# Local attention scores by 64x32 tiles in a windowed attention and sticky-expert kernel

## The chip, the cores and the metric

The kernel runs on one core of one Trainium2 chip. The core has a matrix engine (TensorE, PE in the profile, with its weight loads as PEld), a vector engine (VectorE, DVE), a scalar engine (ScalarE, ACT), GpSimd (POOL), and a queue engine (SyncE, SP) that issues most transfers to 16 DMA engines. Each engine works its own list of instructions in order; semaphores tie the lists together. The metric is device microseconds for one execution.

## The reference

Eight batches of eight heads hold 512 local tokens and 32 global tokens, with 64 features a head. Global tokens attend to all 544 tokens. A local token attends to the 32 global tokens and to the local tokens at most 32 positions away. The attention output, 512 features a token, goes through a mixture of experts, where a token takes its own best expert or, when its gate is at or over one half, that of the token before.

```
s_ll = scale * matmul(q_l, k_l^T);  s_ll = where(|i - j| <= 32, s_ll, -1e9)
s_lg = scale * matmul(q_l, k_g^T)
out_l = softmax([s_lg, s_ll]) @ [v_g, v_l]
out_g = softmax(scale * matmul(q_g, [k_g, k_l]^T)) @ [v_g, v_l]
x = concat(out_g, out_l)          # 8 x 544 tokens of 512
e = argmax(x @ w_gate) if s == 0 or sigmoid(x @ w_local) < 0.5 else e of token s-1
out = softmax(x @ w_gate)[e] * (relu(x @ w1[e]) @ w2[e])
```

## The kernel before, in words

**Units.** `run` (L419) walks 48 units in a fixed order written out by hand: in each batch four local ones (`l`, one pair of heads each) and two global ones (`g`, two pairs each), in the order l0, l1, g0, l2, g1, l3. In step `s` it scores unit `s` and finishes unit `s-2` (transposes of the probabilities, product with v, division). So a step issues on TensorE: the transposes of unit `s-2` (`l_t`, or `g_t`), the scores of unit `s`, and the products with v of unit `s-2`, in two halves for a local unit (`l_av`), with pieces of later work between them (`fpiece`: transposes of finished rows `f1`, the gates `f2`, `f3`).

**Local scores.** The 512 queries are 16 windows of 32. Each window sees 128 keys: its own block, its two neighbours and the global block, and the host's order with a copy on GpSimd (`prep`, L192, the `kx` tile) puts those 128 columns side by side for every window. For one pair of heads, the 128 rows of q and k are 64 features of one head and 64 of the other. To score both heads in one matmul of 128 rows, `prep` copies q into a tile `qbd`, where a window has 64 columns, 32 a head, and the other head's rows are zero. `l_s` (L225) is called twice a unit, for windows 0 to 7 and 8 to 15. Each call writes one PSUM bank: first a bf16 matmul of an identity with a mask (`mask`) that puts a large negative number where a key is out of reach, then eight score matmuls on top of it, each writing 64 of the 128 partitions. `l_max` (L244) takes the row maximum and subtracts it on VectorE, `l_exp` (L251) is the exponential on ScalarE, `l_t` (L255) transposes on TensorE and copies out on ScalarE, and `l_av` (L264) multiplies with v in 16 matmuls of 32 columns, whose last column gives the sum, and divides on VectorE. Scores use a ring of four banks, transposes and outputs two each.

**What a matmul leaves in the profile.** An f32 matmul with another operand than the identity appears as two records, so the 8 score calls of one half are 16 records.

**Transfers.** All loads go through SP's queue in program order. In a local step it issues the load of q and k for the pair after next (`load`, L171, 4224 bytes a partition in a ring of four `raw` buffers that the experts' weights use later), and v for the next pair (`loadv`, L183, 8320 bytes a partition, ring of five). Each is contiguous per partition. A load into a buffer waits for that buffer's last reader, and every later issue on SP waits with it.

**Row store.** When a batch's rows and gate values are done, `f3k` (L398), a generator that VectorE work is dripped from (`drip`, one piece at a few places of each step), computes routing keys and gate probabilities, then waits six further drips (`lag(F4)`, F4 = 6) and calls `f4` (L405), which issues one store of 1056 KB from the row buffer `xa` (ring of two), four of `xg` and one of `gx` on SP. The last batch's store is issued in `tail`.

**Experts.** From step 44 on the first blocks of the expert part begin among the last units (`moe.pre`): gathers, weight loads, and the split of each weight piece into two parts for full precision. Then the blocks run, each a first product (L1158) and a second (L1169), beside the remainder of the attention (`tail`).

Of the kernel before, what the change touches and what calls it, by code (L numbers as in the profile page):

```python
# [11 lines left out]
I32 = mybir.dt.int32  # L12
# [44 lines left out]
F4 = 6  # L57
# [41 lines left out]
class Attn:  # L99
    def __init__(self, tc, cst, tl, at1, at2, raw, ps, qk, qg, vw, xs):  # L100
        nc = self.nc = tc.nc
        self.tc, self.cst = tc, cst
        self.at1, self.at2 = at1, at2
        self.qk, self.qg, self.vw, self.xs = qk, qg, vw, xs
        self.ld = raw
        self.ps_s, self.ps_t, self.ps_o = ps
        self.xa = ring(tl, [P, 4, ROW], F32, "xa", 2)
        self.xg = ring(tl, [P, 2, D], F32, "xg", 2)
# [5 lines left out]
        self.rs = ring(tl, [P, 2, 2, 1], F32, "rs", 3)  # L114
# [6 lines left out]
        self.pt = ring(at1, [P, 4, 2, 2, 32], F32, "pt", 4)  # L121
        self.qbd = ring(at2, [P, NW, 2, 32], F32, "qbd", NBUF)
# [4 lines left out]
        self.mask = at2.tile([P, 8, 2, 32], BF16, name="mask")  # L127
        self.m0 = at2.tile([P, 2, 32], F32, name="m0")
        self.cur = {}
        self.gens = []  # L130
        self.low = 0
        self.banks = False
        self.npr = 0

    def make_mask(self):
# [8 lines left out]
        nc.vector.tensor_copy(self.mask, m0.rearrange("p (o a) k -> p o a k", o=1).broadcast_to([P, 8, 2, 32]))  # L144
        nc.vector.memset(self.mask[0:64, 0, 0, :], NEG)
        nc.vector.memset(self.mask[64:128, 7, 1, :], NEG)
# [24 lines left out]
    def load(self, b, pr):  # L171
# [5 lines left out]
        nc.sync.dma_start(t, self.qk[b, pr])  # L177
# [5 lines left out]
    def loadv(self, b, pr):  # L183
# [3 lines left out]
        nc.sync.dma_start(v.rearrange("p w c -> p (w c)"), self.vw[b, pr])  # L187
# [4 lines left out]
    def prep(self, u):  # L192
# [3 lines left out]
        q = t[:, 0:SL].rearrange("p (w q) -> p w q", q=32)  # L196
        qbd, kx = u["qbd"], u["kx"] = self.qbd(), self.kx()
        k = t[:, SL:]
        kf = kx.rearrange("p m c k -> p (m c) k")
        if self.npr == 0:  # L200
            nc.scalar.copy(out=qbd[0:64, :, 0, :], in_=q[0:64])
            nc.vector.tensor_copy(qbd[64:128, :, 1, :], q[64:128])
            nc.vector.tensor_copy(kx[:, 1:8, 2, :], k[:, 32:64].rearrange("p (o k) -> p o k", o=1).broadcast_to([P, 7, 32]))
        else:
            self.cp(qbd[0:64, :, 0, :], q[0:64], [[0, NW], [0, 32]])
            self.cp(qbd[64:128, :, 1, :], q[64:128], [[0, NW], [0, 32]])
# [7 lines left out]
    def blank(self, i):  # L214
        nc = self.nc
        qbd, kx = self.qbd.t[i], self.kx.t[i]
        nc.vector.memset(qbd[0:64, :, 1, :], 0.0)
        nc.vector.memset(qbd[64:128, :, 0, :], 0.0)
# [6 lines left out]
    def l_s(self, st, hb):  # L225
        nc = self.nc
        if hb == 0:
            b, pr = st["u"]
            if pr == 0:
                self.cur[b]["xa"] = self.xa()  # L230
                self.cur[b]["xg"] = self.xg()
            st["pe"] = self.pe()
        qbd = st["qbd"]
# [3 lines left out]
        nc.tensor.matmul(mo, self.cst.idb, self.mask[:, 4 * hb:4 * hb + 4], start=True, stop=False, skip_group_check=True)  # L237
        for t in range(4):
            for t2 in range(2):
                w = 8 * hb + 2 * t + t2  # L240
                f = 32 * (3 * (w // 2) + w % 2)
                nc.tensor.matmul(sp[64 * t2:64 * t2 + 64, t], qbd[:, w], kf[:, f:f + P], start=False, stop=True, skip_group_check=True)  # L242

    def l_max(self, st, hb):  # L244
        nc = self.nc
        mx = self.mx()
        nc.vector.tensor_reduce(out=mx, in_=st["sp"], axis=AX.X, op=ALU.max)  # L247
        self.drip()
        nc.vector.tensor_tensor(out=st["pe"][:, 4 * hb:4 * hb + 4], in0=st["sp"], in1=mx.broadcast_to([P, 4, P]), op=ALU.subtract)  # L249

    def l_exp(self, st, hb):  # L251
        pe = st["pe"][:, 4 * hb:4 * hb + 4]
        self.nc.scalar.activation(out=pe, in_=pe, func=AF.Exp, scale=SCALE)  # L253

    def l_t(self, st, hb):  # L255
        nc = self.nc
        tp = self.bank(self.ps_t)
        for i in range(4):
            nc.tensor.transpose(tp[:, i], st["pe"][:, 4 * hb + i], self.cst.idf)
        pt = self.pt()  # L260
        nc.scalar.copy(out=pt.rearrange("p i t h q -> p i (t h q)"), in_=tp)
        st["pts"] = st.get("pts", []) + [pt]

    def l_av(self, st, hb):  # L264
# [4 lines left out]
        pt = st["pts"][hb]  # L269
        o = self.ps_o()[:, 0:2 * VW].rearrange("p (g h c) -> p g h c", h=2, c=D + 1)  # L270
        for g in range(2):
            for h in range(2):
                for w4 in range(4):
                    w = 8 * hb + 4 * g + w4
                    nc.tensor.matmul(o[32 * w4:32 * w4 + 32, g, h], pt[:, 2 * g + w4 // 2, w4 % 2, h, :],
                                     v[:, w, h * (D + 1):(h + 1) * (D + 1)], start=True, stop=True, skip_group_check=True)
        rs = self.rs()
        nc.vector.tensor_scalar(out=rs, in0=o[:, :, :, D:D + 1], scalar1=1e-9, scalar2=None, op0=ALU.add)
# [3 lines left out]
        xo = c["xa"][:, 2 * hb:2 * hb + 2, 2 * D * pr:2 * D * (pr + 1)].rearrange("p g (h c) -> p g h c", c=D)  # L282
        nc.vector.tensor_tensor(out=xo, in0=o[:, :, :, 0:D], in1=rs.broadcast_to([P, 2, 2, D]), op=ALU.mult)
# [114 lines left out]
    def f3k(self, b, rt):  # L398
# [3 lines left out]
        yield from lag(F4)  # L402
        self.f4(b, rt)
# [15 lines left out]
    def run(self, rt, moe):  # L419
# [31 lines left out]
        for s in range(n):  # L451
            nx = units[s]
# [23 lines left out]
            if nl:  # L476
                self.l_s(nx, 0)
# [7 lines left out]
            if nl:  # L485
                self.l_exp(nx, 0)
                self.l_s(nx, 1)
# [17 lines left out]
            if s < 6:  # L505
                self.drip(4)
            moe.pre(s - n)
# [11 lines left out]
        self.drip(1000)  # L519
        moe.tail = self.tail(units[n - 2], units[n - 1], fin, rt, moe)  # L520
# [66 lines left out]
class Route:  # L587
# [4 lines left out]
    def setup(self):  # L592
# [6 lines left out]
        i128 = c.tile([P, P], I32, name="i128")  # L599
# [6 lines left out]
        ik = c.tile([P, NF, E], I32, name="ik")  # L606
# [4 lines left out]
        nl = c.tile([P, P], F32, name="nl")  # L611
# [17 lines left out]
        self.o1 = c.tile([P, NT, P], BF16, name="o1")  # L629
        self.oe = c.tile([P, CA, 2, 2 * NX], BF16, name="oe")  # L630
# [728 lines left out]
def _layout(q_l, k_l, v_l, q_g, k_g, v_g, moe_w_gate, moe_w_local, moe_w1, moe_w2):  # L1359
# [5 lines left out]
    r["qk"] = np.concatenate([tr(q_l), tr(k_l)[..., :32], tr(k_g), tr(k_l)[..., 32:]], axis=3)  # L1365
    g = tr(q_g).transpose(0, 2, 1, 3).reshape(B, 2, D, NP, 1, SG)
# [10 lines left out]
    r["vw"] = np.concatenate(rows, axis=2).reshape(B, NP, P, NW * VW)  # L1377
# [31 lines left out]
```

## Time and profile before

| | |
|---|---|
| median of 3 runs | 744.25 us (742.75 to 746.08) |
| the profiled execution's own time | 743.35 us |
| its span, first to last instruction | 741.6 us |
| TensorE busy | 698.0 us (94%) |
| VectorE busy | 503.9 us (68%) |
| ScalarE busy | 411.6 us (55%) |
| GpSimd busy | 238.1 us (32%) |
| moved by DMA | 178.74 MB, mean 241 GB/s |

Busy time is a mean over the attention part and the expert part, which have different limits. A group in a view is written as line, engine, operation, output<-input tile, shape and count; after the bar stand busy time in us, mean length of one in ns, and the engine's idle time before the group with what ended it. For a matmul, `128*64` is rows by columns of the array that the stationary operand takes, and `128x128` the moving operand. Matmuls overlap, so the distance between two starts says more than the printed length.

### The profile page before, as it was taken

How to read it: one execution, taken by the hardware profiler on the slowest of the kernel's cores; microseconds unless marked ns; L12 is line 12 of the kernel's file. 1: busy time of each engine (PE TensorE's matmuls, PEld its weight loads, DVE VectorE, ACT ScalarE, POOL GpSimd, SP SyncE). 2: the span in 40 equal slices, each digit the busy share in tenths (PEclk: the TensorE clock that was granted, in tenths of full speed). 3: DMA queues.
4: the chain of work that ended last, by engine and by line, in shares of the span. 5: the costliest groups of instructions: out<-in, count | busy, mean ns of one | idle time of the engine just before them, and what ended most of it. 6: DMA issues, size and time to landing. Idle time of an engine off the chain costs nothing. (4 is left out here: it accounts for less than half of the span.)

```text
span 741.6 us, 19626 instructions
## 1 busy us (share of the span) xinstructions
PE 698.0 (94%) x7797; PEld 593.0 (80%) x7797; DVE 503.9 (68%) x1207; ACT 411.6 (55%) x724; POOL 238.1 (32%) x333
## 2 busy tenths in 40 slices
PE   9999999999998988899899999999999999999990
PEld 7777777777677877788889888888888988999880
DVE  7877777779887578876558585575858455745560
ACT  4555555554556744545466665566767445645550
POOL 7534434424244455332041412123232121112120
PEclk9999999999999999999999999999999999999995
DMA  8876786767583775677478797757878667657772
GB/s 325 351 260 235 291 312 240 281 245 271 208 323 121 260 246 196 217 248 208 162 238 295 256 299 237 233 191 244 287 238 289 225 221 235 199 193 243 217 228 75
DMA packets 50575, 178.74 MB, mean 241 GB/s; under 512 B 8733, under 2 KB 10013, under 8 KB 46368
## 3 DMA queue, kind: packets, MB, share of 16 engines
q1 hardware_dynamic: 43456, 155.76, 61.4%
q0 software_dynamic: 6720, 21.36, 8.3%
q8 instruction: 71, 1.16, 0.6%
q14 instruction: 40, 0.33, 0.2%
q10 hardware_dynamic: 288, 0.13, 0.1%
HBM read 158.84 MB, written 19.42 MB: 240 GB/s over the span
## 5 line engine op out<-in xcount | busy, mean ns | idle before, releaser
L1097 DVE TENSOR_TENSOR wp<-raw,wp 128x1024 fp32r<-128x1024 f32 x158 | 198.3, 1262 | 8.4 <-ACT wp L1088 8.1
L1088 ACT CAST wp<-raw 128x1024 fp32r<-128x1024 f32 x176 | 182.8, 1048 | 36.5 <-DMA raw<-in_w_dram 34.3
L1169 PE MATMUL ps<-wp,hh 128*128 128x512 f32 x608 | 195.1, 402 | 0.0
L1158 PE MATMUL ps<-xh,wp 128*128 128x256 f32 x1088 | 157.4, 286 | 14.4 <-DVE hl L1161 7.8
L1158 PEld LDWEIGHTS ps<-xh,wp 128*128 128x128 f32 x1088 | 142.3, 192 | 19.1 <-DVE hl L1161 9.4
L1161 DVE SCALAR_TENSOR_TENSOR hl<-ps,hh 128x256 fp32r<-128x256 f32 x136 | 57.1, 422 | 122.7 <-ACT hh L1160 122.7
L1169 PEld LDWEIGHTS ps<-wp,hh 128*128 128x128 f32 x608 | 109.3, 188 | 21.6
L1112 POOL DMA_INDIRECT xr<-xs,idx x46 | 59.5, 1294 | 207.4 <-PE ps L1123 112.8
L1169 PE MATMUL ps<-wp,hl 128*128 128x512 f32 x304 | 120.3, 396 | 0.0
L1160 ACT ACTIVATE hh<-ps 128x256 fp32r<-128x256 f32 x136 | 51.3, 385 | 85.5 <-PE ps L1158 80.6
L1158 PE MATMUL ps<-xl,wp 128*128 128x256 f32 x544 | 87.8, 284 | 0.0
L1179 POOL DMA_INDIRECT out_dram<-y,tk x38 | 40.8, 1074 | 135.5 <-POOLq L1292 28.9
L190 POOL TENSOR_SCALAR_AFFINE_SELECT qbd<-raw 64x512 f32<-64x512 f32 x62 | 44.5, 717 | 120.5 <-PE ps L242 100.3
L1158 PEld LDWEIGHTS ps<-xl,wp 128*128 128x128 f32 x544 | 75.4, 192 | 0.0
L242 PE MATMUL ps<-kx,qbd 128*64 128x128 f32 x1024 | 71.3, 280 | 1.9 <-issue 1.7
L1169 PEld LDWEIGHTS ps<-wp,hl 128*128 128x128 f32 x304 | 57.1, 188 | 13.6
L242 PEld LDWEIGHTS ps<-kx,qbd 128*64 128x64 f32 x1024 | 55.1, 137 | 12.5 <-issue 8.2
L247 DVE TENSOR_REDUCE mx<-ps 128x4 f32<-128x512 f32 x64 | 43.9, 686 | 29.0 <-PE ps L242 28.8
L253 ACT ACTIVATE pe<-pe 128x512 f32<-128x512 f32 x64 | 40.8, 637 | 29.2 <-DVE pe L249 29.2
L1178 ACT ACTIVATE y<-ps,pp 128x512 f32<-128x512 f32 x38 | 26.0, 685 | 52.6 <-issue 46.3
L1097 POOL TENSOR_TENSOR wp<-raw,wp 128x1024 fp32r<-128x1024 f32 x17 | 43.8, 2578 | 23.5 <-ACT wp L1088 22.1
L249 DVE TENSOR_TENSOR pe<-ps,mx 128x512 f32<-128x512 f32 x64 | 44.1, 688 | 1.6
(214 smaller groups left out, 842.3 us busy)
## 6 DMA issues: line engine op xcount, KB each, us to landing
raw<-in_w_dram SPq DMA_DIRECT2D x179, 512.0 KB, 4.5
v<-in_vw_dram SPq DMA_DIRECT2D x32, 1040.0 KB, 9.5
raw<-in_qk_dram SPq DMA_DIRECT2D x32, 528.0 KB, 7.3
xs<-xa SPq DMA_DIRECT2D x8, 1056.0 KB, 4.8
qgb<-in_qg_dram SPq DMA_DIRECT2D x8, 128.0 KB, 3.8
xr<-xs,idx POOLq DMA_INDIRECT x46, 6.3
out_dram<-y,tk POOLq DMA_INDIRECT x38, 5.4
xs<-xg SPq DMA_DIRECT2D x32, 16.0 KB, 4.0
```

Source lines behind the costliest of these rows:

```text
L190: self.nc.gpsimd.affine_select(out=out, in_=in_, pattern=pat, compare_op=ALU.is_ge, fill=0.0, base=0, channel_multiplier=0)
L242: nc.tensor.matmul(sp[64 * t2:64 * t2 + 64, t], qbd[:, w], kf[:, f:f + P], start=False, stop=True, skip_group_check=True)
L247: nc.vector.tensor_reduce(out=mx, in_=st["sp"], axis=AX.X, op=ALU.max)
L249: nc.vector.tensor_tensor(out=st["pe"][:, 4 * hb:4 * hb + 4], in0=st["sp"], in1=mx.broadcast_to([P, 4, P]), op=ALU.subtract)
L253: self.nc.scalar.activation(out=pe, in_=pe, func=AF.Exp, scale=SCALE)
L1088: nc.scalar.copy(out=hi, in_=raw)
L1097: (nc.gpsimd if pool else nc.vector).tensor_tensor(out=lo, in0=raw, in1=hi.bitcast(F32), op=ALU.subtract)
L1112: self.nc.gpsimd.indirect_dma_start(out=self.xr[j], out_offset=None, in_=src, in_offset=bass.IndirectOffsetOnAxis(ap=self.rt.idx[:, 2 * i ...
L1158: nc.tensor.matmul(ph, a[:, dc, fs], b_[:, dc], start=(n == 0), stop=(n == 11))
L1160: nc.scalar.activation(out=self.hh[:, fc], in_=ph, func=AF.Relu)
L1161: nc.vector.scalar_tensor_tensor(out=self.hl[:, fc], in0=ph, scalar=0.0, in1=self.hh[:, fc].bitcast(F32), op0=ALU.max, op1=ALU.subtract)
L1169: nc.tensor.matmul(py, a[:, fc, js], b_[:, fs], start=(fc == 0 and k == 0), stop=(fc == 7 and k == 2))
```

## The change

**Scores by 64x32 tiles.** `qbd` and its copies and zero fills are gone. `l_s` is called once a unit and writes two banks, one a head, each after its own mask matmul. It then makes 32 calls, window by window and head by head: 64 rows (one head's features, read from q where it was loaded), 32 columns (one window's queries), 128 moving columns (the window's keys). A bank now holds one head's 16 windows, four by partition and four along the bank, where it held eight windows of both heads. `l_max`, `l_exp`, `l_t` and `l_av` go by head instead of by half of the windows; the shapes on VectorE and ScalarE stay 128x512 and 128x256. The mask tile is half as long. Within a step the scores of both heads come before the first product with v.

**Row store.** `f4` is no longer called by the generator. At the end of the probabilities the batch is noted with a step, the present one plus F4[b], 4 for batches 0 to 3 and 0 for 4 to 6, and at the end of a step the stores that are due are issued. `xa` and `xg` get three buffers.

**Layout by the host.** q and k of a pair lie in DRAM as two blocks of 128 x 528 floats (2112 bytes a partition each) instead of rows of 4224 bytes, v as four blocks of 128 x 520 floats (2080 bytes). Each load is still one instruction, and the tiles on chip are filled as before.

**Room.** Three scratch tiles of the routing set-up (`i128`, `nl`, `ik`) move into the tile `o1`, which is filled later.

```diff
-F4 = 6
+F4 = (4, 4, 4, 4, 0, 0, 0)
...
         t = c[("qk", pr)] = self.ld()
-        nc.sync.dma_start(t, self.qk[b, pr])
+        nc.sync.dma_start(t.rearrange("p (c x) -> p c x", c=2), self.qk[b, pr].rearrange("c p x -> p c x"))
...
-        nc.sync.dma_start(v.rearrange("p w c -> p (w c)"), self.vw[b, pr])
+        nc.sync.dma_start(v.rearrange("p (g w) c -> p g (w c)", g=4), self.vw[b, pr].rearrange("g p x -> p g x"))
...
-            self.cp(qbd[0:64, :, 0, :], q[0:64], [[0, NW], [0, 32]])
-            self.cp(qbd[64:128, :, 1, :], q[64:128], [[0, NW], [0, 32]])
...
-        sp = st["sp"] = self.bank(self.ps_s)
-        mo = sp.rearrange("p t (k c) -> p t k c", c=32)[:, :, 0::3, :]
-        nc.tensor.matmul(mo, self.cst.idb, self.mask[:, 4 * hb:4 * hb + 4], start=True, stop=False, skip_group_check=True)
+        sp = st["sp"] = [self.bank(self.ps_s) for _ in range(2)]
+        for h in range(2):
+            mo = sp[h].rearrange("p t (k c) -> p t k c", c=32)[:, :, 0::3, :]
+            nc.tensor.matmul(mo, self.cst.idb, self.mask, start=True, stop=False, skip_group_check=True)
         for t in range(4):
-            for t2 in range(2):
-                w = 8 * hb + 2 * t + t2
-                f = 32 * (3 * (w // 2) + w % 2)
-                nc.tensor.matmul(sp[64 * t2:64 * t2 + 64, t], qbd[:, w], kf[:, f:f + P], start=False, stop=True, skip_group_check=True)
+            for h in range(2):
+                r = slice(D * h, D * h + D)
+                for j in range(4):
+                    w = 4 * t + j
+                    f = 32 * (3 * (w // 2) + w % 2)
+                    nc.tensor.matmul(sp[h][32 * j:32 * j + 32, t], q[r, 32 * w:32 * w + 32], kf[r, f:f + P], start=False, stop=True, skip_group_check=True)
...
         yield from rt.probs(b, c["L"], c["xa"])
-        yield from lag(F4)
-        self.f4(b, rt)
+        self.post.append((self.step + F4[b], b))
...
             if nl:
-                self.l_s(nx, 0)
+                self.l_s(nx)
                 self.l_max(nx, 0)
...
             if nl:
                 self.l_exp(nx, 0)
-                self.l_s(nx, 1)
                 self.l_max(nx, 1)
...
+            while self.post and self.post[0][0] <= s:
+                self.f4(self.post.pop(0)[1], rt)
             moe.pre(s - n)
```

More of the change, by code (lines that the diff above doesn't have):

```diff
@@ L126, in __init__ @@
         self.qgb = ring(at2, [P, NP, 2, 32], F32, "qgb", 2)
-        self.mask = at2.tile([P, 8, 2, 32], BF16, name="mask")
+        self.mask = at2.tile([P, 4, 2, 32], BF16, name="mask")
         self.m0 = at2.tile([P, 2, 32], F32, name="m0")
@@ L133, in __init__ @@
         self.npr = 0
+        self.step = 0
+        self.post = []
     def make_mask(self):
@@ L268, in l_av @@
         v = c["v"][pr]
[L269 to L276, printed above, removed]
+        pt = st["pts"][h]
+        o = self.ps_o()[:, 0:4 * (D + 1)].rearrange("p (t c) -> p t c", c=D + 1)
+        for t in range(4):
+            for j in range(4):
+                nc.tensor.matmul(o[32 * j:32 * j + 32, t], pt[:, t, j], v[:, 4 * t + j, h * (D + 1):(h + 1) * (D + 1)],
+                                 start=True, stop=True, skip_group_check=True)
         rs = self.rs()
-        nc.vector.tensor_scalar(out=rs, in0=o[:, :, :, D:D + 1], scalar1=1e-9, scalar2=None, op0=ALU.add)
+        nc.vector.tensor_scalar(out=rs, in0=o[:, :, D:D + 1], scalar1=1e-9, scalar2=None, op0=ALU.add)
         self.drip(hold=True)
@@ L451, in run @@
         for s in range(n):
+            self.step = s
             nx = units[s]
```

75 lines of the change are left out of this document (36 added, 39 removed).

## The prediction

> **What bounds the kernel now.** I read the page's first part, then a table of stretches, then TensorE's own order of work, then waits and transfers. The kernel has an attention part and an expert part; they meet where the last local score starts, 231.8 us by its group:
>
> ```profile
> L242 PE MATMUL ps<-kx,qbd x1024: 269/273/477, 5.4 to 231.8; 128*64 128x128 f32 x171
> ```
>
> The stretches come first; their columns are the length, each engine's busy time, the granted clock, the DMA engines' busy share, and GB/s.
>
> ```profile
> span 741.6 us, 19626 instructions
> PE 698.0 (94%) x7797; PEld 593.0 (80%) x7797; DVE 503.9 (68%) x1207; ACT 411.6 (55%) x724; POOL 238.1 (32%) x333
> ```
> ```profile
> 0.00:12.00 12.00, 10.44 (x94) 8.42 (x96) 8.92 (x24) 3.50 (x5) 9.20 (x34) 1.00 0.84 325
> 12.00:40.00 28.00, 27.39 (x590) 20.80 (x593) 23.37 (x83) 16.99 (x38) 17.86 (x55) 1.00 0.79 309
> 40.00:160.00 120.00, 119.53 (x2542) 90.98 (x2532) 90.59 (x306) 67.95 (x159) 45.66 (x99) 1.00 0.76 280
> 160.00:232.00 72.00, 67.58 (x1373) 51.28 (x1370) 59.47 (x217) 39.44 (x90) 25.92 (x51) 1.00 0.65 239
> ```
>
> From 40 to 160 us TensorE is busy 119.5 of 120 us: it sets the pace. VectorE is second, at 90.6 (75%). From 160 to 232 us VectorE is at 59.5 of 72 (83%) and TensorE has already 4.4 us free. A count of the score records puts 17 pairs of heads into the first stretch and 9 into the second, here with busy time of TensorE and of its weight loads:
>
> ```profile
> 40.00:160.00 120.00, 37.20 (x544) 29.00 (x544) 1.00 0.76 280
> 160.00:232.00 72.00, 19.85 (x288) 15.35 (x288) 1.00 0.65 239
> ```
>
> 32 records are one pair (8 calls for each of two halves, two records a call). What one step costs TensorE is read from its order of work; the time of a group is the distance from its start to the next start, since the printed length includes a tail under which the next group runs.
>
> ```profile
> 106.69 0.33 PE L338 MATMUL ps<-v,ptg 128*32 128x65 f32 x9
> 106.95 1.09 PE L259 MATMUL ps<-idf,pe 128*128 128x128 f32 x8
> 107.88 0.27 PE L237 MATMUL ps<-mask,idb 128*128 128x256 bf16 x1
> 108.08 1.09 PE L242 MATMUL ps<-kx,qbd 128*64 128x128 f32 x16
> 109.10 0.67 PE L275 MATMUL ps<-v,pt 128*32 128x65 f32 x32
> 109.70 0.28 PE L237 MATMUL ps<-mask,idb 128*128 128x256 bf16 x1
> 109.92 1.09 PE L242 MATMUL ps<-kx,qbd 128*64 128x128 f32 x16
> 110.94 0.67 PE L275 MATMUL ps<-v,pt 128*32 128x65 f32 x32
> 111.53 0.87 PE L327 MATMUL ps<-idf,pg 128*128 128x128 f32 x6
> ```
>
> Eight transposes that fill the array take 107.88 - 106.95 = 0.93 us, 0.116 each for 128 moving columns. Sixteen scores, each on half the array's columns, take 109.10 - 108.08 = 1.02 us, 0.064 each: two column halves run at a time. A step has two such runs, 2.04 us, and two masks (0.20 and 0.22 us).
>
> **The scores.** The edit turns 8 + 8 calls of 128 rows by 64 columns, with half of their stationary operand zero, into 32 calls of 64 rows by 32 columns: 64 records a pair instead of 32, each still streaming 128 columns. Alone, one after another, they would take 64 x 0.116 = 7.4 us. What matters is how many run together. The nearest rows are those with 32-column tiles:
>
> ```profile
> 13.01 1.12 PE L275 MATMUL ps<-v,pt 128*32 128x65 f32 x64
> ```
> ```profile
> 219.03 1.06 PE L366 MATMUL ps<-xT,wgl 128*32 128x512 f32 x8
> 219.91 0.64 PE L275 MATMUL ps<-v,pt 128*32 128x65 f32 x32
> ```
>
> Eight gate records of 512 columns would take 8 x 4 x 0.116 = 3.7 us singly and take 0.88: four at a time, nothing lost. And 64 value records last 1.12 where 32 last 0.67, so a further 32 cost 0.45 us, 0.014 each; alone one costs 0.116 x 65/128 = 0.059: again four. No row shows tiles that share columns but not rows, so the cost is bounded: if only the four column tiles overlap, 64/4 x 0.109 + 0.15 = 1.9 us (a run of 1.02 us holds 8 rounds of two; I take 0.109 a round and 0.15 for ramp and change of shape); if all eight do, 8 x 0.109 + 0.15 = 1.02 us. I take eight: in the rows both two and four tiles side by side reach their full number, the halves of rows hold different heads, and they write different banks (each head has its own). That removes one run: -1.02 us a pair, -32.7 us in 32 pairs; with four it would be -0.15 a pair.
>
> [...]
>
> **Around the scores.** One more row, of POOL's copies of q:
>
> ```profile
> L190 POOL TENSOR_SCALAR_AFFINE_SELECT qbd<-raw 64x512 f32<-64x512 f32 x62 | 44.5, 717 | 120.5 <-PE ps L242 100.3
> ```
>
> The two masks follow each other, so one change of tile shape goes: 0.20 + 0.22 becomes about 0.11 + 0.21, -0.1 a pair, -3.2 us. The two value runs can stand together where no finishing piece falls between them: 0.60 + 0.59 becomes 0.45 + 0.60, -0.15 in about half of the steps, -2.4 us. At the start the second pair's keys no longer wait behind two POOL copies of q (0.72 us each); about -1. Together TensorE sheds 39 us, 1.2 a pair.
>
> **What is late next: VectorE.** Its work a pair does not change: the maximum, the subtraction and the scaling keep their shapes.
>
> ```profile
> L249 DVE TENSOR_TENSOR pe<-ps,mx 128x512 f32<-128x512 f32 x34 | 23.5, 692 | 1.0
> L247 DVE TENSOR_REDUCE mx<-ps 128x4 f32<-128x512 f32 x34 | 23.4, 688 | 18.7 <-PE ps L242 18.7
> L283 DVE TENSOR_TENSOR xa<-ps,rs 128x256 f32<-128x256 f32 x35 | 14.8, 422 | 2.1 <-DMA xs<-xa 1.3
> ...
> L280 DVE RECIPROCAL rs<-rs 128x4 f32<-128x4 f32 x35 | 6.2, 178 | 0.7
> L278 DVE TENSOR_SCALAR rs<-ps 128x4 f32<-128x4 f32 x35 | 5.4, 155 | 1.2 <-PE ps L275 0.9
> ```
>
> From 40 to 160 us TensorE needs 120 - 17 x 1.2 = 99.6 us, against 90.6 for VectorE. In a step with both a local pair to score and one to finish, VectorE has 4 x 0.69 + 2 x 0.75 = 4.3 us beside its small pieces and TensorE now about 4.0 (3.3 and a finishing piece), in steps of the global rows it is the other way round; four banks of scores let one engine run about a step ahead. I charge 3 us: 102.6, a gain of 17.4. From 160 to 232 us TensorE would need 67.6 - 10.8 = 57 us, less than VectorE's 59.5; at 95% VectorE takes 62.6, a gain of 9.4. Before 40 us VectorE (32.3 of 40) allows about 4. The sum is -30.8 before transfers, 8 us less than TensorE alone gives.
>
> **Store and descriptors.** The row store waits in SP's queue for VectorE, and each load behind it waits too:
>
> ```profile
> 52.37 0.38 SPq L187 DMA_DIRECT2D v<-in_vw_dram  x1
> 63.62 0.38 SPq L412 DMA_DIRECT2D xs<-xa  x1
> 64.06 3.22 SPq L416 DMA_DIRECT2D xs<-xg  x4
> 67.37 0.37 SPq L417 DMA_DIRECT2D xs<-gx  x1
> 67.85 1.39 SPq L177 DMA_DIRECT2D raw<-in_qk_dram  x1
> ```
> ```profile
> SPq L412 <- DVE xa L768: 47.2, 5, 11.5
> SPq L1077 <- PE ps L295: 14.3, 2, 9.0
> ```
> ```profile
> POOL qbd L190 <- PE ps L242: 100.3, 23, 8.0
> POOL qbd L190 <- DMA raw<-in_qk_dram: 11.7, 4, 4.3
> ```
>
> No load leaves between 52.4 and 67.9 us; POOL then waited four times for keys (11.7 us), but had 100 us to spare, and TensorE did not stop. So the move earns 0 by itself (up to 2 if it ends small waits), and is cover: with shorter steps the same hold would reach TensorE, at up to 4.3 us a batch. Batches 0 to 3 move four steps back, so the six issues of each store (one row, four xg, one gx, 4 us of SP) stand behind finished data; a third row buffer pays for that. Batches 4 to 6 lose the six drips of delay they had, so SP waits for VectorE as before or longer, with the next q, k and v queued behind. I charge 1 us (0 to 3 x 3).
>
> Descriptors:
>
> ```profile
> v<-in_vw_dram SPq DMA_DIRECT2D x32, 1040.0 KB, 9.5
> raw<-in_qk_dram SPq DMA_DIRECT2D x32, 528.0 KB, 7.3
> xs<-xa SPq DMA_DIRECT2D x8, 1056.0 KB, 4.8
> ```
>
> The row store moves 1056 KB as rows of 528 floats, 2.1 KB each, and lands in 4.8 us, v with its 8.3 KB rows in 9.5: pieces of 2 KB carry this rate, so 0. At the other end, as many bytes in less time raise the DMA share from 0.76 to about 0.76 x 120/103 = 0.89; from there a load can be late. POOL loses 44.5 us of copies that it hid anyway. TensorE now reads q in the loaded buffer, which is free one use later: the fourth weight load waited for the global scores (L295) and will wait for the last local scores, a step later, with the other weight loads behind it. Price 0 to 3 us, taken as 1. The sum: -30.8 + 1 + 1 = -28.8.
>
> **The rivals.** (1) The likeliest: eight tiles at a time, VectorE close behind. 743.35 (the profiled execution, span 741.6) - 28.8 = 714.5; it lies 0.9 under the median of 744.25, so 715.4 for a median; own range 707 to 722. (2) VectorE binds harder: its waits for scores (18.7 of 120 us) stay as they are, because each maximum must follow its scores. Then 90.6 + 18.7 = 109.3 us instead of 120; that 9% over 192 us is 17, with the start 18: 726. For it: VectorE is 83% busy in the second stretch; against: half of its waits are for a second run that goes. [...] (3) The row halves don't overlap: -0.15 - 0.1 - 0.07 a pair, -10 us: 734. Against: side-by-side tiles overlap in full; for: no row shows it. (4) Full gain, both engines hidden: -39: 705. (5) The slower side: going from one row half to the other empties the array, as a change of shape does. The row of the mask gives the price: 0.20 us to the next start for work of 0.11, so 0.09 lost. Sixteen rounds of 0.109 + 0.09 make 3.2 us where two runs took 2.04, +1.15, less 0.17 around them, +1.0 a pair: +31 us, 775. It decides from about 30 ns a change. Against it: all 64 value records run through four tiles without such a gap, though within one set of rows.
>
> **How the numbers follow.** Chances: (1) 0.52, (2) 0.14, (3) 0.13, (4) 0.09, (5) 0.09, and 0.03 that late loads or late weights take back a small gain. The time is that of (1), 715. The range 702 to 736 takes in (1) to (4), 0.88 less their edges. About 0.5% (3.7 us) is what can be told from no change: faster 0.87 (cases 1 to 4 but for an edge), same 0.04, slower 0.09.
>
> **What would show it.** The order of work after: one group of 64 score records in 1.0 us (four at a time: 1.9; emptying: over 3), two masks together, steps about 1.2 us shorter on TensorE, the last score record at about 202 us instead of 231.8. VectorE above 85% from 40 us until there, its waits for scores well below 0.55 us each. SP without a hold of 15 us in batches 0 to 3. The expert part unchanged to about 3 us. I am wrong if the score group takes over 1.3 us, if VectorE stays near 75% while TensorE has gaps, or if TensorE waits for POOL's keys after loads.

## The result, and the profile after

The changed kernel takes 771.27 us (median of 4 runs, 767.73 to 774.64) where the kernel before takes 745.16 (4 runs, 742.75 to 753.18): 1.034 times as long, 95% interval 1.027 to 1.041. The forecast was 715. A profile is of one execution, which can be longer than its kernel's median: 774.64 us here, and further on 756.75 (two new units, median 753.08), 843.88 (split loads, 842.07) and 747.93 (nearly no loads, 738.2). The span of this one is 31.2 us longer than that of before. Most of this lies ahead of the expert part: the last local score starts at 257.6 us instead of 231.8, and what follows it takes 515.2 us instead of 509.8.

The page of the changed kernel, its first lines, the granted clock in 40 slices of the span, and the queue that brings the engines' code:

```profile
span 772.8 us, 21648 instructions
...
PE 684.2 (89%) x8821; PEld 579.1 (75%) x8821; DVE 497.7 (64%) x1202; ACT 410.2 (53%) x723; POOL 194.2 (25%) x271
...
PEclk9999899889999997999999999999999999999996
...
q8 instruction: 79, 1.29, 0.7%
```

TensorE has less busy time than before (684.2 against 698.0) and 1024 matmul records and 1024 weight loads more, 64 instructions a pair. The page of before has this line for the code:

```profile
q8 instruction: 71, 1.16, 0.6%
```

Eight packets more for 2048 more instructions: a packet is a block of 256 TensorE instructions, 1.29 MB / 79 = 16 KB. The stretches of the changed kernel, in the columns of the prediction's table:

```profile
12.00:40.00 28.00, 21.48 (x683) 16.70 (x685) 19.43 (x74) 15.29 (x37) 9.59 (x41) 1.00 0.86 316
40.00:160.00 120.00, 95.88 (x2458) 70.39 (x2455) 72.53 (x257) 56.43 (x133) 17.84 (x52) 0.90 0.66 226
160.00:232.00 72.00, 59.23 (x1662) 44.37 (x1660) 55.73 (x209) 35.86 (x83) 13.14 (x36) 0.95 0.67 229
```

Before, TensorE was busy for 119.5 of the 120 us from 40 to 160; now for 95.9, and VectorE has become emptier with it, 72.5 instead of 90.6. Neither is the bound. What TensorE waits for, between 6 and 258 us (us in total, times, longest):

```profile
PE ps L238 <- issue: 12.9, 7, 4.1
PE ps L269 <- issue: 12.9, 7, 3.5
PE ps L332 <- issue: 4.8, 2, 3.0
PE ps L345 <- DVE xa L277: 4.8, 4, 2.5
```

and the largest entry of the same view of before, 6 to 250 us:

```profile
PE ps L242 <- issue: 1.7, 2, 1.3
```

"issue" is idle time in which the engine waits for nothing that the profile shows. It sits in front of the scores (L238), the products with v (L269) and the global products (L332), the lines with the smallest matmuls, and it is 30.6 us in these three rows. TensorE's order of work shows what such a wait looks like, and beside it a step without one:

```profile
44.51 0.38 PE L231 MATMUL ps<-mask,idb 128*128 128x256 bf16 x2
44.82 0.89 PE L238 MATMUL ps<-kx,raw 64*32 64x128 f32 x43
49.82 0.99 PE L238 MATMUL ps<-kx,raw 64*32 64x128 f32 x21 [4.11 <-issue]
...
59.72 0.38 PE L231 MATMUL ps<-mask,idb 128*128 128x256 bf16 x2
60.03 1.16 PE L238 MATMUL ps<-kx,raw 64*32 64x128 f32 x64
61.12 1.35 PE L269 MATMUL ps<-v,pt 128*32 128x65 f32 x64
```

Sixty-four score records take 61.12 - 60.03 = 1.09 us, as forecast. But the group before stops after 43 records, in the middle of an operation whose operands are all there, and goes on 4.1 us later. In the stretch from 47.3 to 48.4 us, inside this gap, the transfers' view has one instruction packet in a stream of loads:

```profile
DMA packets 204, 0.42 MB, mean 377 GB/s; under 512 B 13, under 2 KB 13, under 8 KB 203
## 3 DMA queue, kind: packets, MB, share of 16 engines
q1 hardware_dynamic: 203, 0.40, 97.9%
q8 instruction: 1, 0.02, 5.0%
```

**TensorE has run out of instructions.** The following is worked out from the single records of the trace, by counting all of TensorE's instructions in it (matmuls, weight loads and the few of its sequencer) from the start and setting the instruction packets beside the count. In both traces a block's packet begins some time after a mark that returns every 256 instructions, and lasts about 1.0 us (0.9 to 1.4). Where TensorE used up the 256 from that mark before the packet had landed, it stopped, each time at the same remainder of the count (193), and went on 1.3 to 1.5 us after the packet's end. Up to 225 us that happens once before the change and 12 times after it (in two of the 12 the packet had landed less than 0.1 us earlier). From the first instruction after the mark to the packet it is 2.2 us in the mean before (5.3 at most) and 2.6 after (6.6 at most). After the change, the waits of over 3 us stand where loads move 240 to 405 GB/s between mark and packet, and with no load in that time it is 0.4 to 1.6 us. The expectations below count from the last instruction before the mark, which takes in a stop at the mark itself; by that count the means are 2.3 and 3.4, and the longest is 7.9.

So the wait itself has grown little. What the change has cut is the time that it must fit into, and that is in the tables: before, 2542 + 2532 records in 120 us are a block every 6.05 us. In the new step (mask, 64 scores, 64 values, with their weight loads) 256 records last about 3 us. A wait of 2.6, a transfer of 1.0 and the 1.4 until TensorE goes on are 5.0 us, which fit into the first and not into the second.

The granted clock falls with the stops: 0.90 from 40 to 160 us, and 1.00 before. In the trace's single clock records it is 1.00 or 0.50; ahead of the last score 0.50 comes in stretches of 3.4 or 6.8 us, 34.1 us in all, and none before the change. Each stretch at half clock begins inside a stop or at most 1.2 us after one.

### The profile page after: what moved, and what is told of

It is laid out like the page before. It is cut to its first block, busy times and chain, and to the rows that moved or that the text cites. A ratio compares the mean times of both kernels' runs of the same rounds, so it can differ in the third digit from the quotient of the medians.

```text
span 772.8 us, 21648 instructions
## 1 busy us (share of the span) xinstructions
PE 684.2 (89%) x8821; PEld 579.1 (75%) x8821; DVE 497.7 (64%) x1202; ACT 410.2 (53%) x723; POOL 194.2 (25%) x271
## 3 DMA queue, kind: packets, MB, share of 16 engines
q8 instruction: 79, 1.29, 0.7%
## 5 line engine op out<-in xcount | busy, mean ns | idle before, releaser
L1167 PE MATMUL ps<-wp,hh 128*128 128x512 f32 x608 | 197.4, 406 | 0.0
L192 POOL TENSOR_SCALAR_AFFINE_SELECT kx<-raw 128x384 f32<-128x384 f32 (+3 forms) x127 | 44.1, 372 | 188.4 <-PE ps L238 131.1
L269 PE MATMUL ps<-v,pt 128*32 128x65 f32 x2048 | 44.4, 231 | 19.6 <-issue 12.9
L269 PEld LDWEIGHTS ps<-v,pt 128*32 128x32 f32 x2048 | 35.9, 115 | 29.7 <-issue 19.5
L238 PE MATMUL ps<-kx,raw 64*32 64x128 f32 x2048 | 42.0, 280 | 13.0 <-issue 12.9
L1095 POOL TENSOR_TENSOR wp<-raw,wp 128x1024 fp32r<-128x1024 f32 x17 | 43.1, 2539 | 21.1 <-ACT wp L1086 18.3
```

What stands on the lines that cost most here:

```text
L192: self.nc.gpsimd.affine_select(out=out, in_=in_, pattern=pat, compare_op=ALU.is_ge, fill=0.0, base=0, channel_multiplier=0)
L238: nc.tensor.matmul(sp[h][32 * j:32 * j + 32, t], q[r, 32 * w:32 * w + 32], kf[r, f:f + P], start=False, stop=True, skip_group_check=True)
L269: nc.tensor.matmul(o[32 * j:32 * j + 32, t], pt[:, t, j], v[:, 4 * t + j, h * (D + 1):(h + 1) * (D + 1)], start=True, stop=True, skip_grou ...
L1095: (nc.gpsimd if pool else nc.vector).tensor_tensor(out=lo, in0=raw, in1=hi.bitcast(F32), op=ALU.subtract)
L1167: nc.tensor.matmul(py, a[:, fc, js], b_[:, fs], start=(fc == 0 and k == 0), stop=(fc == 7 and k == 2))
```

## The experiments

In the expectations theory A is the one of the section above: more instructions, a block of code that waits behind loads, and a TensorE that runs out of them. Its rivals are named where they stand.

**The parts one by one.** Scores alone, with the old layout and the old store:

```diff
-        nc.sync.dma_start(t.rearrange("p (c x) -> p c x", c=2), self.qk[b, pr].rearrange("c p x -> p c x"))
+        nc.sync.dma_start(t, self.qk[b, pr])
...
-        nc.sync.dma_start(v.rearrange("p (g w) c -> p g (w c)", g=4), self.vw[b, pr].rearrange("g p x -> p g x"))
+        nc.sync.dma_start(v.rearrange("p w c -> p (w c)"), self.vw[b, pr])
...
-        self.post.append((self.step + F4[b], b))
+        yield from lag(6)
+        self.f4(b, rt)
```

> The new scores alone, with q, k and v in pieces of 4 and 8 KB and the row store six drips after the probabilities as before. Theory A (TensorE runs out of instructions: 64 score records a pair with as many weight loads, where there were 32 of each, use up a 16 KB instruction block faster than the next one arrives behind the loads): gaps of 2 to 4 us ended by nothing the profile shows stay, over 20 us of them before the last score, 760 to 775 us. Theory B (the 2 KB pieces delay the instruction blocks): the gaps go, 712 to 725 us. Theory C (the moved store collides with loads): 712 to 725 us as well.

Scores and store with the old layout (the first half of that edit):

> The whole change but for the layout by the host: q, k and v in pieces of 4 and 8 KB. Theory A: 760 to 775 us, gaps as after the change. Theory B: 712 to 725 us. Theory C: about 770 us. The mean wait of an instruction block tells what the pieces do to it: shorter with large pieces by B, the same by A.

Scores and layout with the old store (the second half):

> The whole change but for the row store, which comes six drips after the probabilities as before. Theory A: 760 to 780 us, and the hold of 10 to 15 us in SP's queue is back, so the bursts of loads behind it are larger. Theory B: about 770 us. Theory C: 712 to 730 us.

The kernel before with the new layout alone (the two load lines and the host's reshaping):

> The kernel before with nothing but the layout by the host: pieces of 2 KB. Theory A: within 4 us of the kernel before, since its TensorE uses up an instruction block in 6 us. Theory B: gaps of over 1 us appear, 755 us or more. Theory C: no change.

In the table, a ratio is to executions of the kernel before from the same session, and a block counts as used up when the last of the 256 instructions begins before the next packet has landed or at most 0.1 us after.

| kernel | median us | ratio to before, 95% | last local score, us | block used up, up to 225 us |
|---|---|---|---|---|
| before | 745.16 | 1 | 231.8 | 1 |
| layout only | 743.03 | 0.998 (0.994 to 1.001) | 231.2 | 1 |
| scores only | 761.18 | 1.023 (1.017 to 1.029) | 247.2 | 9 |
| scores and layout | 766.9 | 1.030 (1.024 to 1.036) | 248.4 | 9 |
| scores and store | 774.4 | 1.042 (1.035 to 1.049) | 256.8 | 12 |
| all three | 771.27 | 1.034 (1.027 to 1.041) | 257.6 | 12 |

The scores alone make the kernel slower, with waits of the same kind (scores only, TensorE, 6 to 258 us):

```profile
PE ps L238 <- issue: 13.7, 7, 4.7
PE ps L269 <- issue: 7.3, 5, 2.2
PE ps L332 <- issue: 4.7, 2, 2.4
```

The layout is worth nothing that can be measured. The store's move costs 774.4 - 761.2 = 13 us with the old layout, where the intervals lie apart. With the new one the difference is 771.3 - 766.9 = 4 us, the intervals overlap, and a cost isn't shown. Its kernels have three more used-up blocks each. Why it makes more of them no run settles.

**Fewer instructions or fewer loads.** If the code is late, either a smaller need for it or a freer way must help. With half as many score calls, each of two windows (odd windows are scored against the keys of the even one beside them), the instructions are as many as before the change:

```diff
-                for j in range(4):
-                    w = 4 * t + j
-                    f = 32 * (3 * (w // 2) + w % 2)
-                    nc.tensor.matmul(sp[h][32 * j:32 * j + 32, t], q[r, 32 * w:32 * w + 32], kf[r, f:f + P], start=False, stop=True, skip_group_check=True)
+                for j in range(2):
+                    w = 4 * t + 2 * j
+                    f = 32 * 3 * (w // 2)
+                    nc.tensor.matmul(sp[h][64 * j:64 * j + 64, t], q[r, 32 * w:32 * w + 64], kf[r, f:f + P], start=False, stop=True, skip_group_check=True)
```

> The whole change with scores in 64x64 tiles: one call for two windows, 16 calls a pair instead of 32, so 32 records and 32 weight loads as before the change, with the same tiles side by side (four of 64 columns, where there were eight of 32) and the same time on the array, near 1.0 us a pair. The odd windows are scored against the keys of the even ones, so the output isn't the reference's. Theory A (too many instructions a microsecond): the gaps of over 2 us go or nearly, 712 to 730 us. Theory D (row halves or q read from the load buffer hold TensorE up): 760 to 775 us.

The second takes loads away: only the first five v are loaded, and later pairs use what stands in the buffers.

```diff
-        nc.sync.dma_start(v.rearrange("p (g w) c -> p g (w c)", g=4), self.vw[b, pr].rearrange("g p x -> p g x"))
+        if self.v.k <= NV:
+            nc.sync.dma_start(v.rearrange("p (g w) c -> p g (w c)", g=4), self.vw[b, pr].rearrange("g p x -> p g x"))
```

> The whole change without the loads of v after the first five: later pairs use the v of earlier ones, so the output isn't the reference's. 27 of 32 loads of 1040 KB are left out. Theory A with the queue (a block waits behind the loads in flight): mean wait of a block from 3.4 us to under 2, gaps from 47 us to under 20, 715 to 735 us. Theory A without it (a block takes that long by itself): gaps stay near 45 us, 760 to 775 us.

And both together:

> Both remedies together: scores in 64x64 tiles (16 calls a pair) and no loads of v after the first five, so the output isn't the reference's. Theory A: with as many instructions as before the change and blocks that wait less, gaps from 47 us to under 20, 712 to 728 us, that is the time that the prediction's sum gave. If something else holds the kernel (VectorE, the moved store, q read from the load buffer), it stays at 738 us or more, with gaps under 20 us but VectorE or POOL behind them.

Where data is changed, other tokens go to other experts, and the expert part has another length (480 to 517 us after the last local score in these runs, 515 in the changed kernel); so these runs are read by the time of the last score. It comes at 235.6 us with half the calls, 245.9 with few v, 221.6 with both, against 257.6 in the changed kernel; used-up blocks are 4, 7 and 2, and the mean wait for a block with few v is 2.0 us, where it was 2.6. The totals are 741.28, 747.76 and 723.01 us: those of the two single edits lie between the ranges of theory A and of its rivals, in neither, and that of both lies in the range expected. Half the calls left the products with v, 128 instructions in a row:

```profile
PE ps L269 <- issue: 11.1, 8, 3.4
PE ps L345 <- DVE xa L277: 5.7, 4, 2.6
PE ps L238 <- issue: 3.5, 3, 1.9
```

The wait in front of the scores fell from 12.9 to 3.5 us; that in front of the values, whose number is unchanged, stayed at 11. These two rows hold 14.6 us with as many instructions as before the change, where the kernel before waited 1.7: what counts here is not the number of instructions but the number in a given time, and products with v that stood in two runs now stand in one. Each edit takes part of the stall, as the theory wants, and neither all of it.

**Instructions added to the kernel before.** If the number of instructions is enough, the kernel before must stall too when it gets more of them. Thirty-two matmuls of one column a pair, into a column that nobody reads, add 128 instructions a pair (64 matmul records and 64 weight loads). That is twice what the change adds, not as many, as the expectation has it:

```diff
         bank = self.ps_o()
         o = bank[:, 0:2 * VW].rearrange("p (g h c) -> p g h c", h=2, c=D + 1)
+        for k in range(16):
+            j = k % 4
+            nc.tensor.matmul(bank[32 * j:32 * j + 32, 500:501], pt[:, 0, 0, 0, :], v[:, 0, 0:1], start=True, stop=True, skip_group_check=True)
```

> The kernel before with 32 more matmuls of one moving column a pair, in 32-column tiles, written to an unused column of the output's bank: as many more instructions as the change adds (64 records and 64 weight loads a pair) with the old scores. By the 14 ns of a value record they cost TensorE up to 0.9 us a pair, 29 us. Theory A: gaps ended by nothing the profile shows grow from 7 us to over 15 us and an instruction block is used up to its last instruction in several places, 765 to 800 us. If the new tiles are what stalls TensorE, gaps stay under 10 us and the time is 745 to 775 us.

It took 795.79 us (1.072, 1.065 to 1.079), with 87 packets of code, 8 used-up blocks, and this (TensorE, 6 to 250 us, then the stretch):

```profile
PE ps L279 <- issue: 11.3, 7, 2.8
PE ps L242 <- issue: 5.2, 5, 1.5
PE ps L274 <- issue: 3.4, 3, 1.7
```
```profile
40.00:160.00 120.00, 108.43 (x2882) 83.36 (x2884) 71.82 (x243) 55.05 (x127) 36.18 (x79) 0.96 0.57 208
```

The scores of this kernel are the old ones, and it stalls ahead of them (L242, 5.2 us instead of 1.7) and ahead of the values (L279). New tiles are not needed for it, only more instructions, though here twice as many more. The last score came 47 us later than before. Where the code is there, an added run takes 0.28 us:

```profile
65.42 0.43 PE L274 MATMUL ps<-v,pt 128*32 128x1 f32 x32
65.70 0.66 PE L279 MATMUL ps<-v,pt 128*32 128x65 f32 x32
```

Two runs a pair in 32 pairs make 18 us, the three rows of waits 20, and 17.1 us at half clock cost up to 8.5 (an estimate, half of their length): 46 of the 47.

**The new scores in some pairs only.** One of four local units a batch with the new scores, then two, with `NEWU = (0, 2)`; `l_s2` holds the scores of the changed kernel, and the other units keep the old form:

```diff
+NEWU = (0,)
...
+        new = u["new"] = pr in NEWU
...
+        if st["new"]:
+            if hb == 0:
+                self.l_s2(st, kf)
+            return
```

> The kernel before with the new scores in one local unit of four (the first of each batch, eight pairs), old layout, old store. Theory A: the instructions of a batch grow by 5%, TensorE still uses up a block more slowly than it arrives, gaps under 12 us, 8 x 1.2 us saved: 733 to 741 us. If the new tiles stall by themselves, a quarter of the loss: 748 to 753 us.

> The same with the new scores in two local units of four (first and third, 16 pairs). Theory A: at the edge between the two limits; 16 x 1.2 us saved against gaps of 10 to 25 us: 732 to 750 us. If the new tiles stall by themselves, half of the loss: 752 to 760 us.

747.52 us (1.007, 1.004 to 1.010) and 753.08 (1.013, 1.007 to 1.019); used-up blocks 2 and 8. Both were expected to gain and did not. The second lies in the range named for tiles that stall by themselves, the first just under it, so by their totals these two runs speak for that rival and not for theory A's sum. What speaks against the rival is the run with nearly no loads below. With one unit in four the last score is at 234.0 us, 2 us late. The ratio rises with the number of new units, from 1 by 1.007 and 1.013 to the 1.023 of scores only; neither mixture wins.

**Where v is issued, and how far ahead.** Issuing v from ScalarE's queue, or with a ring of four v buffers instead of five, moves the loads in time but not their bytes. The first:

```diff
-        nc.sync.dma_start(v.rearrange("p (g w) c -> p g (w c)", g=4), self.vw[b, pr].rearrange("g p x -> p g x"))
+        nc.scalar.dma_start(v.rearrange("p (g w) c -> p g (w c)", g=4), self.vw[b, pr].rearrange("g p x -> p g x"))
```

> The whole change with the loads of v issued by ScalarE, in its order of work, instead of SP, which issues up to two of v and two of q and k at once. 32 issues of about 0.4 us on ScalarE, which is half idle. Theory A with the queue: smaller bursts, mean wait down by 0.5 to 1.5 us, 735 to 760 us. Theory A without it: 765 to 775 us.

The second:

```diff
-NV = 5
+NV = 4
```

> The whole change with four buffers for v instead of five, so that a load of v waits for the product of three pairs before, and SP can't issue its loads in one burst. Theory A with the queue: mean wait down by 0.3 to 1 us, 745 to 765 us, unless loads now come late for v, which TensorE would show as waits at the products with v. Theory A without it: 765 to 780 us.

778.06 us (1.043, 1.036 to 1.050) and 777.52 (1.041, 1.031 to 1.051), the mean wait for a block 2.6 and 2.7 us, as in the changed kernel: no help, against the expectation. The first lies above both of its ranges, the second in the one for blocks that don't wait behind loads. Neither way of moving the loads in time shortened the wait.

**Loads split into 120 and 8 partitions.** On the scores-only kernel, this was to show whether a block waits on one particular DMA engine. That the large part leaves one engine free was the author's assumption; no trace here shows which engines a load uses. The edit:

```diff
+        for r in (slice(0, 120), slice(120, P)):
+            nc.sync.dma_start(t[r], self.qk[b, pr][r])
...
+        for r in (slice(0, 120), slice(120, P)):
+            nc.sync.dma_start(v.rearrange("p w c -> p (w c)")[r], self.vw[b, pr][r])
```

> The scores alone (old layout, old store), with each load of q and k and of v issued as 120 partitions and 8 partitions, so that the large part may use 15 of the 16 DMA engines. If an instruction block is held by the loads on one DMA engine that is the last one, its mean wait falls from 3.1 us to under 1 us, gaps from 41 us to under 20, 715 to 735 us. If it is another engine, or a wait that all share, the wait stays near 3 us: 758 to 775 us, with 64 issues more on SP.

842.07 us (1.120, 1.108 to 1.132). That is outside both ranges. The split loads are slow in themselves, and keep the engines busier (12 to 40 us; the same stretch of scores only moved 311 GB/s at a busy share of 0.78):

```profile
12.00:40.00 28.00, 18.30 (x425) 13.17 (x424) 12.28 (x42) 10.18 (x25) 6.66 (x32) 0.82 0.97 217
```
```profile
PE ps L240 <- issue: 22.9, 7, 5.6
PE ps L271 <- issue: 21.0, 9, 4.8
PE ps L334 <- issue: 10.3, 3, 5.4
```

A block now waits 4.2 us in the mean, where it waited 2.4 with scores only. That says that with busier DMA engines the code comes later, but not on which engine it waits, so the question it was made for stays open.

**Nearly no loads.** The sharpest test of the theory keeps the whole change and its instructions, and takes the loads away: v for the first five pairs, q and k for the first four, later pairs reuse them.

```diff
+        if 4 * b + pr < 4:
+            nc.sync.dma_start(t.rearrange("p (c x) -> p c x", c=2), self.qk[b, pr].rearrange("c p x -> p c x"))
...
+        if self.v.k <= NV:
+            nc.sync.dma_start(v.rearrange("p (g w) c -> p g (w c)", g=4), self.vw[b, pr].rearrange("g p x -> p g x"))
```

> The whole change without the loads of v after the first five and of q and k after the first four, so the output isn't the reference's; only the row stores and small loads stay. By the queue: mean wait of a block under 2 us against 3.4, three or fewer places where a block is used up, last score record before 235 us (257.6 with all loads). If blocks are slow by themselves: wait over 2.5 us, last score record after 245 us.

The same with half the score calls as well:

> The same with scores in 64x64 tiles (16 calls a pair), so the output isn't the reference's: as many instructions as before the change and hardly any load. What is left is what the prediction counted: last score record at 200 to 212 us if its sum (202) holds; at 215 to 222 us if the waits of TensorE for VectorE at the output banks, 16 us with v left out, are the rest.

With the full number of instructions (stretch, and TensorE's waits from 6 to 240 us):

```profile
40.00:160.00 120.00, 109.80 (x3262) 83.46 (x3257) 92.56 (x336) 72.53 (x171) 24.59 (x72) 1.00 0.14 47
```
```profile
PE ps L347 <- DVE xa L279: 8.6, 7, 2.5
PE ps L271 <- DVE xa L279: 7.9, 8, 2.3
PE ps L271 <- issue: 2.6, 2, 2.2
PE ps L240 <- issue: 2.0, 3, 1.4
```

The mean wait for a block is 1.3 us, two blocks are used up (at 17 us, among the first loads, and at 217), TensorE takes 3262 + 3257 records in 120 us, a block every 4.7 us, at full clock, and waits 4.6 us for code instead of 30.6. The last score starts at 229.3 us: 28 us of the changed kernel's time are gone, and nothing in the computation's instructions was changed. Batches 2 to 5 take 25.8 to 26.7 us each, from first score to first score, where they took 27.8 to 28.9 before the change and take 32.0 to 35.5 with all loads. Its median is 738.2 us (0.990, 0.987 to 0.993).

With half the calls too (701.28 us) no block is used up, and the last score comes at 218.1 us; batches 2 to 5 take 25.7 to 25.9 us. The 11 us between the two runs arise mostly in the other batches; the one with all instructions has 20.5 us at half clock there, this one 6.8. What is left of TensorE's waiting is VectorE:

```profile
40.00:160.00 120.00, 107.59 (x2681) 81.99 (x2680) 94.21 (x336) 72.74 (x170) 24.95 (x73) 1.00 0.17 56
```
```profile
PE ps L347 <- DVE xa L279: 10.0, 7, 2.9
PE ps L271 <- DVE xa L279: 8.3, 8, 2.3
```

Transposes of finished rows (L347) and products with v (L271) wait for the division of the pair before (L279), 18.3 us in all, while VectorE is busy for 94.2 of 120 us.

## Why the prediction was wrong

**The scores.** "I take eight" was right: 1.09 us a group of 64 against the 1.02 of the working, by rows 60.03 and 61.12. So is the sum for the two masks (0.31 us) and, where the code is there, for the value runs: from 62.30 to 63.35 us in the kernel with few loads, 1.05 us for 64 records. Rival 3 (row halves that don't overlap, 1.9 us) and rival 5 (emptying, 3.2 us a group) are out by the same rows. Rival 5's 775 us is near the measured time, but nothing of its mechanism is there.

**The step that failed** is the next sentence, "That removes one run: -1.02 us a pair, -32.7 us in 32 pairs", and with it "From 40 to 160 us TensorE needs 120 - 17 x 1.2 = 99.6 us". It counted 64 records a pair and priced them by the time of the array alone. The 64 instructions a pair that come in addition (weight loads and matmuls) were given no price, and the same instructions were to be used in less time. The page of before had the row that was missing from the argument: 71 packets of code, 16 KB each, which it counts on the same 16 DMA engines, 76% busy already from 40 to 160 us. The trace of before shows one used-up block, at about 190 us, and blocks that land with 9 to 24 records to spare at 29, 35 and 115 us. The forecast's own pace, 64 more instructions a pair in 102.6 us instead of 120, is (5074 + 17 x 64) / 102.6 = 60 records a us, a block every 4.3 us in the mean and 3 within a step, against the 2.6 + 1.0 + 1.4 = 5.0 us of a block after the change, from its mark until TensorE goes on.

What stood in its place: with the code in time (few loads, half the calls, where the scores take 1.04 us a pair, from 65.72 to 66.76) 231.8 - 218.1 = 13.7 us of the gain of 30 are there, and from that run to the changed kernel 257.6 - 218.1 = 39.5 us are lost. The three rows of waits for code hold 30.6 us, and 34.1 us at half clock cost up to 17 (an estimate, half of their length). How these two divide the loss can't be separated here, because the half clock follows the stops and partly lies in them. That the cause is late code, and not the tiles, is shown from both sides: the old scores with more instructions stall, and the new ones with few loads hardly do. That the code is late behind loads is shown by the loads taken away; by what path they hold it up is not.

**What is late next.** "I charge 3 us" for VectorE was too little. With the code in time (few loads, half the calls) the last score is at 218 us and not at the forecast 202, and TensorE waits 18.3 us for VectorE's divisions. VectorE does not reach the 85% or more forecast from 40 us on; it is at 94.2 / 120 = 79%. The place differs too: it holds TensorE by the division that frees an output bank, not by the maxima of the scores. Rival 2 had the right engine, and nearly its price by luck, since the wait that it counted is another: 17 us gained by 232 us in its working, 13.7 in this run.

**Store.** "So the move earns 0 by itself ... I charge 1 us (0 to 3 x 3)" was wrong in size with the old layout, 13 us; the 4 us with the new one are within the noise. The move did shorten the hold at the store. SP's waits before, over the whole span:

```profile
SPq L177 <- PE ps L295: 57.2, 8, 16.0
SPq L412 <- DVE xa L768: 47.2, 5, 11.5
...
SPq L412 <- DVE gx L771: 26.8, 2, 15.6
```

and after:

```profile
SPq L179 <- PE ps L289: 111.2, 11, 15.6
...
SPq L179 <- PE ps L238: 13.7, 6, 4.3
SPq L405 <- DVE gx L769: 13.3, 1, 13.3
...
SPq L405 <- DVE kg L800: 7.1, 1, 7.1
...
SPq L405 <- DVE xa L766: 4.7, 1, 4.7
```

For the store SP waits 13.3 + 7.1 + 4.7 = 25.1 us in these rows instead of 74.0. For the q and k buffer, which the global scores (L289, before L295) and now also the local ones (L238) release, it waits 111.2 + 13.7 = 124.9 us instead of 57.2. So the waiting has moved and not gone, and loads leave together when that buffer comes free. Five left before the stall of 4.1 us shown above, in SP's order of work:

```profile
40.96 0.37 SPq L179 DMA_DIRECT2D raw<-in_qk_dram  x1
...
42.90 0.52 SPq L189 DMA_DIRECT2D v<-in_vw_dram  x1
57.07 0.37 SPq L179 DMA_DIRECT2D raw<-in_qk_dram  x1
```

They move 2 x 528 + 128 + 2 x 1040 KB in all, and the next load leaves 14 us later.

**Descriptors** at 0: right (0.998). The expert part "unchanged to about 3 us": 5.4 us longer, with 17 us of half clock where there were 7. Of the signs named in advance, "VectorE stays near 75% while TensorE has gaps" came true at 60% (40 to 160 us).

**Still open** are why a block waits up to 6.6 us behind loads (one engine's backlog or all of them), why the store's move adds stalls, and the share of the half clock. Of all the versions run, none with the full computation is measurably faster than the kernel before.

## What to carry to other kernels

Before matmuls are cut smaller, count TensorE's instructions as well as its array time: weight loads and matmuls, divided by the time they are to take, give the us a block of 256 has, and that has to cover the wait for the next one, its transfer and the time until TensorE goes on (here 2.6 in the mean and up to 6.6, 1.0 and 1.4 us, with loads in flight most of the time). Here the gap of 4.1 us marked "issue", in the middle of a group whose operands were ready, was a wait for code; look for an instruction packet inside such a gap. To tell a short supply of code from everything else, take the loads away and leave the instructions as they are.

## What the runs showed of the hardware that was not expected

- TensorE stopped in the middle of a group, at the same remainder of its instruction count each time (193 of 256), and went on about 1.4 us (1.3 to 1.5) after a 16 KB packet had landed. The packet took 0.9 to 1.4 us.
- From the mark of the count to the next packet it was, in the changed kernel, 0.4 to 1.6 us where no load was in flight, 2.6 in the mean of all and up to 6.6.
- In the changed kernel the granted clock was 1.00 or 0.50, and its changes lay multiples of 3.4 us apart. The eight windows of that length ahead of the last score that were followed by one at half clock had TensorE idle for 58 to 96% of their length (gaps of over 0.25 us between the starts of matmuls); of the 55 that were followed by full clock the idlest had 61%. So a window that was idle only in part was enough here, and the two ranges overlap.
- Sixty-four records of tiles of 64 rows by 32 columns, over 128 moving columns, took 1.09 us, 0.017 each, where a transpose that fills the array took 0.116 before (eight in 0.93 us). That is 6.8 times the pace; with the 0.15 us that the prediction allows for ramp and change of shape taken off it is 7.9, which agrees with eight tiles at a time (an estimate from these numbers).
- Loads split into 120 and 8 partitions kept the DMA engines 97% busy at 217 GB/s, where the same kernel with whole ones moved 311 GB/s at 78% (12 to 40 us).
